# Batch 1's q and k loaded in runs of 72 tokens

## The chip, the cores and the metric

One core of a Trainium2 chip runs the whole program. The time is device microseconds of one execution; a kernel's time is the median over its runs. The engines are TensorE (PE; its weight loads, which overlap its matmuls, are listed as PEld), Vector (DVE), ScalarE (ACT), GpSimd (POOL) and SyncE (SP). Data moves between memory and the core by DMA, issued here from GpSimd's queue (all loads that change type on the way, fp32 to bf16) and from SyncE's.

## The reference

Causal attention with a forget-like bias, then a token mixer of rank 32 and a two-layer channel mixer. Inputs q, k, v are (8, 8, 576, 64): batch, heads, tokens, head size.

```python
scores = scale * np.matmul(q, k.transpose(0, 1, 3, 2))
s_pos = np.maximum(s, 0.0)
cum = np.cumsum(s_pos, axis=-1)
bias = -(cum[:, :, :, None] - cum[:, :, None, :])
scores = np.where(causal, -1000000000.0, scores + np.minimum(bias, 0.0))
attn = softmax(scores)                      # by rows, + 1e-09 in the sum
x = (attn @ v) as (batch, token, 512)
xt = x.transpose(0, 2, 1)
h = xt @ U @ V                              # (512, 576) @ (576, 32) @ (32, 576)
u = x + h.transpose(0, 2, 1)
return u + np.maximum(u @ w_ch1, 0.0) @ w_ch2
```

## The kernel before

The attention goes by pairs of heads: pair n = 4b + hp is pair hp of batch b, and there are 32. A pair has three steps, each a generator that is advanced piece by piece. `transposes(n)`, T_n for short, turns q and k of the pair: TensorE multiplies [72 x 128] pieces by an identity into PSUM, and copies (L337 or L340) bring them to a buffer `slot`, head size along the partitions, tokens along the free axis. `scores(n)`, S_n, multiplies k by q from the slot into PSUM (L404), ScalarE takes the exponential (L419, L430, L436) into `pT`, and a mask sets the causal part to zero. `values(n)`, V_n, multiplies pT by v (L464) and divides by the sum of the row (L473, L474). `seqmix(b)`, M_b, is the token mixer of one batch, and `chanmix(g)` the channel mixer for 512 tokens, with its first product on line L650 and its second on L660 or L699.

TensorE is kept busy by filling the attention's waits with pieces of `chanmix`. From pair 4 to pair 9 the order is written out by hand as words: "T4 T4", then "S4 T5 S4 T5 ...", then "V4 V4 S7 V5 ..." and so on, a piece of `chanmix` between them at a set pace. From pair 8 on it comes from a loop. In the end the order of TensorE's and GpSimd's instructions is fixed as written. Vector's, ScalarE's and SyncE's orders are fixed through batch 0 alone; after that a scheduler sets them.

How q and k come in. One tile of q and one of k per batch, 72 partitions x 8 heads x 512 numbers, with two buffers in turn. `load_qk(b, h, n)` loads n heads from h on, q and k each by one DMA from GpSimd's queue. `in_runs(b, h)` says which of two forms it takes, and the copies of `transposes` ask it too.

- In rows (L119): partition p holds tokens 8p to 8p + 7. For one head these lie side by side in memory, 2,048 B of fp32, and are written as 1,024 B of bf16. Turned on TensorE, the tokens come out in steps of 8, and the copies (L340) put each into its place: the source is read in steps of 72 elements, and every second element of the destination is written.
- In runs (L114): partition p holds tokens p, 72 + p, 144 + p and so on. Each piece is one token, 256 B of fp32 written as 128 B. Turned, each of the eight groups is a run of 72 tokens in their order, and the copies (L337) read and write runs of 72.

Before the change, batch 0, batch 1 and heads 0 to 3 of batch 2 are loaded in rows, heads 4 to 7 of batch 2 and all later batches in runs.

Where batch 1's loads stand. GpSimd issues in the order written. Heads 0 to 3 of batch 1 (q, then k) are issued at about 17.2 us, after the masks of pair 0 and before the masks of pair 1, w1's second half (L270), and the masks of pairs 2 and 3. Heads 4 to 7 are issued at about 25.8 us, after those masks; then follow w2's first half (L275), batch 1's v in five parts (L188), w2's second half, batch 2's q and k in two halves, and batch 2's v. The consumers of these on TensorE: T4 at 34.5 us, T6 at 43.5, the second product of `chanmix(0)` (L660) from 50.7, V4 at 53.0, T8 at 61.0.

Of the kernel before, what the change touches and what calls it, by code (L numbers as in the profile page):

```python
# [39 lines left out]
def kernel(  # L40
# [15 lines left out]
    B, H, S, D = q.shape  # L56
# [49 lines left out]
        k_t[b] = loads.tile([TP, H, TT * D], BF16, tag="k_sd", name="k_sd")  # L106

    def in_runs(b, h):
        return b > 2 or b == 2 and h >= 4

    def load_qk(b, h, n):
        for dst, src in ((q_t[b], q), (k_t[b], k)):
            if in_runs(b, h):
                nc.gpsimd.dma_start(  # L114
                    out=dst[:, ds(h, n), :].rearrange("p h (t d) -> p (h t) d", t=TT),
                    in_=src[b, ds(h, n)].rearrange("h (t p) d -> p (h t) d", p=TP),
                )
            else:
                nc.gpsimd.dma_start(  # L119
                    out=dst[:, ds(h, n), :],  # L120
                    in_=src[b, ds(h, n)].rearrange("h (p t) d -> p h (t d)", p=TP),
                )
# [173 lines left out]
    def transposes(n):  # L296
# [30 lines left out]
        for hh in range(2):  # L327
            if b > 0:
                turn(hh, 0)
            turn(hh, 1)  # L330
            tp = tps[hh]
            dst = slot[0:D, hh, 0 : 2 * S]
            for par in range(2):
                src = tp[par * D : par * D + D]
                if in_runs(b, 2 * hp):
                    by_run = dst.rearrange("p (c t two m) -> p c t two m", c=2, t=4, two=2)
                    copies(n, hh, par)(by_run[:, :, :, par, :], src)  # L337
                else:
                    in_turn = dst.rearrange("p (c m t two) -> p c m t two", c=2, t=4, two=2)
                    copies(n, hh, par)(  # L340
                        in_turn[:, :, :, :, par], src.rearrange("p c t m -> p c m t")
                    )
            yield
# [854 lines left out]
    for n in range(2 * PB, NP + 2):  # L1198
        b, hp = divmod(n, PB)
# [97 lines left out]
```

The softmax here doesn't subtract the row's maximum and nothing guards it: scores larger than these inputs give would overflow.

## Time and profile before

| | before |
|---|---|
| median of 14 runs | 363.35 us (362.35 to 369.06) |
| the profiled execution | 365.19 us |
| its span | 363.5 us |
| granted TensorE clock | 1.0 throughout |
| GpSimd's DMA queue | 110,016 packets, 18.50 MB |
| SyncE's and ScalarE's DMA queue | 44,760 packets, 18.64 MB |
| copies of turned q and k, L340 | 29 on Vector, 11 on ScalarE |
| copies of turned q and k, L337 | 76 on Vector, 12 on ScalarE |

The span runs from the first to the last instruction of the profiled execution; what lies around it makes the execution's time. Durations and points of time in this text come from that one execution. Sizes of DMA packets are those written, so bf16 where the load changes type. A DMA's row in the trace covers its issue on the engine; when its data has landed is told beside it.

### The profile page before, as it was taken

To read this page: it belongs to the slowest core of one execution; us is meant where nothing else is said; L and a number is where in the kernel's file an instruction comes from. 1 tells how busy PE (TensorE), PEld (TensorE's weight loads), DVE (VectorE), ACT (ScalarE), POOL (GpSimd) and SP (SyncE) were. 2 spreads that over 40 slices of the span, in tenths; PEclk is the share of its full clock that TensorE was granted. 3 is DMA by queue.
4 is the path that set the end of the run, shared out by engine and by line. 5 is a ranking of instruction groups with operands and counts; after the bars stand their busy time and mean duration, and the time that the engine had idled before them with its cause. 6 is when DMAs were issued, how large, how long until landed. Compare 5 with 4: busy or idle time off the path is not lost.

```text
span 363.5 us, 9613 instructions
## 1 busy us (share of the span) xinstructions
PE 350.4 (96%) x3999; PEld 256.9 (71%) x4039; DVE 276.4 (76%) x604; ACT 213.1 (59%) x322; POOL 84.9 (23%) x108
## 2 busy tenths in 40 slices
PE   8999999999997999999999999999899999999996
PEld 4675566665586667886689667876588548888885
DVE  7876776778787758995799659995697769676674
ACT  3874975846761577347853677348743554675710
POOL 8997161714040402140224003000000000000000
PEclk9999999999999999999999999999999999999999
DMA  7999999999999799959993999254222716010022
GB/s 108 163 195 202 160 178 132 153 143 126 96 108 105 144 132 70 107 76 131 131 85 70 149 148 86 50 119 81 6 29 72 150 20 127 29 60 31 30 88 87
DMA packets 155107, 37.94 MB, mean 104 GB/s; under 512 B 138680, under 2 KB 153432, under 8 KB 155064
## 3 DMA queue, kind: packets, MB, share of 16 engines
q0 software_dynamic: 110016, 18.50, 83.6%
q1 hardware_dynamic: 44760, 18.64, 31.2%
q8 instruction: 31, 0.51, 0.6%
q10 hardware_dynamic: 288, 0.20, 0.2%
q14 instruction: 12, 0.10, 0.1%
HBM read 37.25 MB, written 9.70 MB: 129 GB/s over the span
## 4 chain that ended last, share of the span: by engine, by line
PE 77%; DVE 11%; ACT 4%; DMA 3%; issue 3%; DVEq 0%; ACTq 0%
PE pwork L650 21%; PE pwork L699 11%; PE quarter L699 10%; PE pscore L404 9%; PE pwork L464 7%; PE parts L911 6%; PE pwork L317 4%; PE pwork L660 3%; DMA xT<-x_sb 3%; DVE uT L518 2%; DVE slot L677 2%; ACT hT L1000 2%; ACT pT L419 1%; DVE slot L340 1%; DVE o_sb L713 1%
## 5 line engine op out<-in xcount | busy, mean ns | idle before, releaser
L650 PE MATMUL pwork<-uT,w_sb 128*128 128x512 bf16 x401 | 105.9, 379 | 2.6 <-ACT hT L1000 0.9
L1000 ACT ACTIVATE hT<-pwork 128x512 bf16<-128x512 f32 x108 | 65.1, 607 | 38.4 <-PE pwork L650 38.1
L419 ACT ACTIVATE pT<-pscore 128x1024 bf16<-128x1024 f32 x56 | 56.5, 1029 | 50.8 <-PE pscore L404 50.0
L650 PEld LDWEIGHTS <-w_sb 128*128 128x128 bf16 x448 | 38.3, 98 | 35.9 <-issue 1.3
L404 PE MATMUL pscore<-slot 68*128 68x320 bf16 (+1 forms) x500 | 55.2, 246 | 0.2
L404 PEld LDWEIGHTS <-slot 68*128 68x128 bf16 x564 | 41.2, 97 | 17.0 <-issue 1.3
L699 PEld LDWEIGHTS <-hT 128*128 128x128 bf16 x496 | 46.3, 98 | 7.0 <-DVE uT L518 0.5
L188 POOL DMA_DIRECT2D v_slot<-in_v_dram x36 | 30.3, 854 | 78.3 <-PE pwork L464 67.1
L349 DVE TENSOR_TENSOR pT<-pT,keep 128x512 bf16<-128x512 bf16 (+1 forms) x81 | 28.6, 354 | 21.8 <-ACT pT L419 16.0
L464 PEld LDWEIGHTS <-pT 128*128 128x128 bf16 x870 | 32.4, 98 | 8.0 <-issue 2.9
L337 DVE COPY slot<-pwork 64x576 bf16<-64x576 bf16 x76 | 34.4, 453 | 4.6 <-PE pwork L317 3.7
L464 PE MATMUL pwork<-v_slot,pT 128*128 128x65 bf16 x870 | 35.5, 193 | 2.3 <-DVE uT L518 2.2
L474 DVE TENSOR_TENSOR x_sb<-pwork,rec 128x320 bf16<-128x320 f32 x64 | 31.2, 489 | 1.4
L430 ACT ACTIVATE pT<-pscore 128x1024 bf16<-128x1024 f32 x29 | 30.2, 1041 | 1.7 <-PE pscore L404 1.5
L699 PE MATMUL pwork<-w_sb,hT 128*128 128x256 bf16 x240 | 30.6, 273 | 0.0
L340 DVE COPY slot<-pwork 64x576 bf16<-64x576 bf16 x29 | 23.3, 803 | 5.3 <-PE pwork L317 3.5
L699 PEld LDWEIGHTS <-slot 128*128 128x128 bf16 x256 | 24.0, 98 | 4.6 <-issue 1.6
L114 POOL DMA_DIRECT2D q_sd<-in_q_dram x6 | 12.6, 2107 | 48.2 <-PE pwork L317 35.5
L473 DVE RECIPROCAL rec<-pwork 128x5 f32<-128x5 f32 x64 | 12.1, 190 | 12.7 <-PE pwork L464 12.4
L699 PE MATMUL pwork<-w_sum,slot 128*128 128x256 bf16 x160 | 20.3, 273 | 0.7 <-DVE o_sb L713 0.7
L317 PEld LDWEIGHTS <-q_sd 72*128 72x128 bf16 x256 | 14.8, 99 | 8.6 <-DMA q_sd<-in_q_dram 0.9
L317 PE MATMUL pwork<-identity,q_sd 72*128 72x72 bf16 x256 | 18.2, 198 | 0.1
(165 smaller groups left out, 544.5 us busy)
## 6 DMA issues: line engine op xcount, KB each, us to landing
out_dram<-o_sb SPq DMA_DIRECT2D x35, 256.0 KB
w_sb<-in_moe_w_ch_dram POOLq DMA_DIRECT2D x4, 1024.0 KB, 13.6
v_slot<-in_v_dram POOLq DMA_DIRECT2D x28, 128.0 KB, 10.2
q_sd<-in_q_dram POOLq DMA_DIRECT2D x5, 576.0 KB, 15.4
k_sd<-in_k_dram POOLq DMA_DIRECT2D x5, 576.0 KB, 20.1
q_sd<-in_q_dram POOLq DMA_DIRECT2D x4, 288.0 KB, 13.2
k_sd<-in_k_dram POOLq DMA_DIRECT2D x4, 288.0 KB, 12.8
q_sd<-in_q_dram POOLq DMA_DIRECT2D x4, 144.0 KB, 4.9
```

Of the source, the lines that this page charges most:

```text
L188: nc.gpsimd.dma_start(out=vt[:rows_t, t, :, 0:D], in_=v[b, :, ds(t * 128, rows_t), :].rearrange("h p d -> p h d"),)
L317: nc.tensor.transpose(tps[hh][:, c, t2, :], src[:, 2 * hp + hh, ds(t2 * 128, 128)], identity[:TP, :TP],)
L337: copies(n, hh, par)(by_run[:, :, :, par, :], src)
L349: nc.vector.tensor_tensor(dst, dst, keep[:, :, 0:w].to_broadcast([128, n_tiles, w]), op=ALU.min)
L404: nc.tensor.matmul(dst, lhsT=slot[0:KA, hh, ds(S + j * 128, 128)], rhs=slot[0:KA, hh, lo:hi], start=True, stop=True,)
L419: nc.scalar.activation(pT[:, hh, 0:1024], near, EXP, scale=scale)
L430: nc.scalar.activation(pT[:, :, 1024:1536], mid.rearrange("p (a b) -> p a b", a=2), EXP, scale=scale)
L464: nc.tensor.matmul(po[:, i, :], lhsT=pT[:, hh, ds(place(j, i), 128)], rhs=vt[:, j, h, :], start=(j == 0), stop=(j == i), skip_group_check= ...
L474: nc.vector.tensor_tensor(x_sb[:, hp, :, ds(hh * D, D)], po[:, :, 0:D], rec.to_broadcast([128, 5, D]), op=ALU.mult,)
L650: nc.tensor.matmul(f1, lhsT=w1_sb[:, kt, ds(nf * 128, 128)], rhs=u[:, kt, :], start=(kt == 0), stop=(kt == 3),)
L699: nc.tensor.matmul(acc[:, i, :], lhsT=a[:, kt, ds(i * 128, 128)], rhs=b[:, kt, :], start=(begin and i == 0 and kt == 0), stop=(kt == HF - ...
L1000: nc.scalar.activation(hT[:, nf, :], f1, RELU)
```

## The change

`in_runs` answers yes for all of batch 1 as well. Heads 0 to 3 of batch 2 stay in rows, as batch 0 does.

```diff
     def in_runs(b, h):
-        return b > 2 or b == 2 and h >= 4
+        return b in (1, *range(3, B)) or b == 2 and h >= 4
```

So four DMAs (q and k of heads 0 to 3 and of heads 4 to 7 of batch 1) go from line L119 to L114, each from 288 pieces to 2,304 for the same bytes, and the sixteen copies of T4 to T7 go from L340 to L337. The instructions on TensorE and on GpSimd, and their order, are otherwise the same. On Vector the scheduler puts some of its work around these copies in another order: the three copies of V_sb (L1190), which stood after T4's copies, and the four of V_end (L1191), which stood before them, both come after them, and some masks (L349) change places with the copies of T5 to T7. On SyncE two small transfers of bias rows (L301) change places.

## The prediction

> **What bounds the kernel now.** I read the page's engine row first, then the loads' rates and landings, then the chain and Vector's rows in the stage of the change.
>
> ```profile
> PE 350.4 (96%) x3999; PEld 256.9 (71%) x4039; DVE 276.4 (76%) x604; ACT 213.1 (59%) x322; POOL 84.9 (23%) x108
> DMA  7999999999999799959993999254222716010022
> 34.00:56.00 22.00, 21.52 (x231) 13.36 (x234) 16.35 (x31) 18.62 (x29) 9.47 (x13) 1.00 1.62 174
> ```
>
> TensorE is busy 96% of the span; the DMA digits (slices of 9.1 us) stand at nine from about 9 to 118 us. The third line is the windows view for 34 to 56 us, where batch 1's heads are turned, scored and multiplied: PE idles 22.00 - 21.52 = 0.48 us there, so no cheaper Vector work can give back more than that in this stage. The last figures are a DMA share of 1.62 (over one: packets overlap) and 174 GB/s: the GpSimd queue always has a transfer in hand.
>
> What the edit buys is the price of a copy out of PSUM, L340 (row form) against L337 (run form):
>
> ```profile
> L340 DVE COPY slot<-pwork x29: 786/804/820, 8.3 to 69.1; 64x576 bf16<-64x576 bf16 x29
> L337 DVE COPY slot<-pwork x76: 439/454/459, 78.4 to 267.8; 64x576 bf16<-64x576 bf16 x76
> 52.69 1.63 DVE L340 COPY slot<-pwork 64x576 bf16<-64x576 bf16 x2
> 54.37 1.02 PE L660 MATMUL pwork<-w_sb,hT 128*128 128x512 bf16 x4 [0.26 <-DVE slot L340]
> ```
>
> Minimum/median/maximum are ns. The last two lines are the timeline: the only named TensorE wait on these copies between 34 and 62 us is 0.26 us.
>
> What it costs is seen in the DMA view of two stretches, batch 1's second half (row form, 33.0 to 36.9 us) and batch 2's second half (run form, 58.7 to 64.9 us), and in the landings of the two k loads that bound the second.
>
> ```profile
> DMA packets 853, 0.76 MB, mean 195 GB/s; under 512 B 119, under 2 KB 852, under 8 KB 852
> DMA packets 6152, 0.69 MB, mean 111 GB/s; under 512 B 6146, under 2 KB 6152, under 8 KB 6152
> L119 POOL DMA_DIRECT2D k_sd<-in_k_dram x1: 719/719/719, 43.6 to 43.6; - x1
> DMA to landing us min/median/max: 15.1/15.1/15.1
> L114 POOL DMA_DIRECT2D k_sd<-in_k_dram x1: 1407/1407/1407, 47.8 to 47.8; - x1
> DMA to landing us min/median/max: 17.2/17.2/17.2
> 61.15 0.29 PE L317 MATMUL pwork<-identity,k_sd 72*128 72x72 bf16 x4
> ```
>
> The first number of a landing line is how long after the issue the data was there. The row loads ran at 195 GB/s, the run loads at 111, in the bf16 bytes written. Batch 2's first k half, in rows, landed at 43.6 + 15.1 = 58.7 us; TensorE first reads it at 61.15 us (T8). That slack, 61.15 - 58.7 = 2.4 us, is the number everything turns on. Two other loads are as near: the fifth part of batch 1's v, issued at 33.6, takes 16.8 us to land (50.4 us), and V4 starts at 52.96 us; the second half of w2 lands at 35.7 + 19.5 = 55.2 us and is first wanted near 58.7 us (the seventeenth L660 matmul).
>
> **The change, part by part.** No instruction is added, removed or moved on TensorE; the order on GpSimd is the same too.
>
> Copies. Batch 1 has T4 to T7 with 4 copies each: 14 on Vector, 2 on ScalarE (L340's rows between 34 and 56 us count 14 and 2). Vector saves 14 x (805 - 454) ns = 4.9 us; ScalarE 2 x (798 - 634) ns = 0.3 us. What hides this is TensorE's own work. I take the 0.26 us of the named wait, bounded by 0 and 0.48 us. Vector's order shifts with the scheduler (the three V_sb copies go behind T4's), which has the same cover.
>
> Issues on GpSimd. Four issues change from L119 to L114. A run issue of four heads took 1.43 and 1.41 us, a row issue 0.77 and 0.72: +0.67 us each. The first pair is issued at 17.2 us with no gap to the masks behind it: masks of pT(1), a memset, a w1 load, masks of pT(2) (22.46 to 23.9) and pT(3) (to 25.8) all slide by up to 1.35 us. V2 starts on TensorE at 25.5, where its masks would now end near 25.3; V3 starts at 27.1, its masks would end near 26.9 because the third of them stood 0.29 us waiting for ScalarE. So 0.1 us, bounded by 0 and 0.4. Behind the second pair (25.8 us) stand w2's first half and v of batch 1, 2.5 us later in issue; their landings lie 16 us after issue, behind other transfers, so this costs nothing unless the queue ran dry.
>
> Transfers. Each of the four loads moves the same bytes: 72 partitions x 4 heads as 288 packets of 1,024 B become 2,304 of 128 B. A q and k pair in rows cost the queue, from the landing ahead of it to that of its k: batch 1's second (w1's half at 21.6 + 11.4 = 33.0, k at 26.5 + 10.4 = 36.9) 3.9 us, batch 2's first (w2's half at 55.2, k at 58.7) 3.5, batch 1's first (w1's half at 23.9, k at 17.9 + 9.5 = 27.4) 3.5: mean 3.6. A pair in runs, batch 2's second: 47.8 + 17.2 = 64.9 less 58.7, 6.2 us. So +2.6 us a pair, and D = 5.2 us of delay from two pairs for all that is queued behind. Bounds: batch 4's full k load, the same packets as a pair, landed 4.3 us after its q (86.3 + 23.8 less 84.0 + 21.8), giving +0.7 a pair and D = 1.4; batch 3's (65.9 + 17.8 less 63.5 + 13.2) 7.0 us after its q, giving +3.4 and D = 6.8. The rates say the like of the middle: 294,912 B at 195 and at 111 GB/s are 1.5 and 2.7 us, times four +4.6. I take 5.2, from the same shape in the same queue, nearest in time.
>
> What is late. The first halves would land near 30 us against T4 at 34.5, the second near 42 against T6 at 43.5: no wait. Then all slack is spent. Batch 1's last v part: 50.4 + 5.2 = 55.6 against some 53.3 us (it feeds the last of V4's first fifteen matmuls), a stall of 2.3; w2: 60.4 against 58.7 + 2.3, none; T8's k: 63.9 against 61.15 + 2.3, another 0.5. These are one delay, not three: together D - 2.4 = 2.8 us (0 to 4.4 by the bounds of D), and all of TensorE's order stands behind the waiting matmul, with Vector and ScalarE, which wait for its products. The queue issues one transfer only when the eighth before it has landed (w2's second half, at 35.7, waited for q of batch 1, landed 35.4), so the delay is not made up at the issue.
>
> Afterwards. Batch 3's k lands at 83.7 us against T12 at 88.3: 4.6 us of slack, of which 2.4 would be used. At 105.4 us the last transpose of batch 2's x stands 9.76 us on the chain, TensorE idles 2.24 us for it, and the GpSimd queue works beside it until 118 us. If the loads, 2.4 us later relative to TensorE, push it back, it costs up to 2.4 more; if the two share as before, nothing. I take 0, and 2.4 for the range. After 118 us the queue stands empty until 124, so lateness ends there, but a TensorE stall stays: it idles only 223.0 - 217.1 = 5.9 us in the last 223.
>
> Sum: +2.8 - 0.3 + 0.1 = +2.6 us. The profiled execution is 365.19 us (span 363.5 and 1.7 around it), so 367.8 for its like; it lies 1.84 above the median of the 14 runs, and on 363.35 the sum is 365.9.
>
> A rule to weigh. The Trainium skill, "DMA: Bandwidth & Descriptors", section "Anatomy of one DMA — SWDGE (gpsimd) path", fits a transfer as 2 us plus its bytes over 436 GB/s, whatever its pieces. By that fit rows and runs cost alike, D is 0 and the sum would be some 363.2 us. The same page's "Specifications" ask at least 512 B a transfer for line rate, which speaks against the change. The 195 and 111 GB/s above side with the second, and they decide.
>
> **The rivals.**
>
> Hidden: the delay fits the slack. For it: 2.4 us are free, and batch 4's and 5's k loads come 4.3 and 4.8 us after their q, giving D = 1.4 and 2.4. Against it: those compare landings deep in a backlog, where engines have run ahead. Then TensorE keeps its pace and gains 0 to 0.48: 362.9 to 363.4 us. This is the case that isn't slower; it decides as long as D stays under 2.4.
>
> Doubled: TensorE stalls 2.8 to 4.4 us and the transpose at 105 us is pushed by a further 1 to 2.4. For it: between 106 and 110 us the queue's loads ran and the transpose hardly did. Against: the loads it meets are issued on TensorE's own progress. 363.35 + 2.6 + 1 to 363.35 + 4.2 + 2.4: 367.0 to 370.0 us.
>
> Reordered, faster: the later backlog lets that transpose go first; its 2.24 us wait goes and nothing stalls before. 363.35 - 0.3 - 2.24 = 360.8 us at best. Nothing in the rows asks for it except that 9.76 us is long.
>
> That the change does nothing is excluded: the four issues and sixteen copies carry the other lines.
>
> **How the numbers follow.** The forecast, a stall of 1 to 4.4 us at V4 and T8: 0.57, 364.2 to 367.6 us (363.35 - 0.2 and the stall). Hidden: 0.18. Doubled: 0.17. Reordered: 0.08. The predicted time is the forecast's: 365.9 us. From 363.0 to 368.8 lies all of the first, most of hidden and of doubled; below lie the faster case and the rest of hidden (0.11), above the rest of doubled (0.06). By itself the likeliest case spans 364.2 to 367.6. A measurement of this kernel can tell 0.2%, 0.7 us, from no change: faster means under 362.6, slower over 364.1. Slower is the first and third, 0.74, with a hair of hidden, 0.75; same, most of hidden, 0.15; faster 0.10.
>
> **What would show it.** Right: batch 1's k landings some 2.5 and 5 us later than 27.4 and 36.9 us; batch 2's first k at about 64 us; TensorE waiting for a DMA by name, at V4 or T8, in a stretch where it had none; the copies at 455 ns. Wrong: no DMA wait there (the step D fails), masks on GpSimd holding V2 or V3 (the 0.1 fails), or a gain in 34 to 56 us over 0.48 us, which would mean that TensorE's modelled busy time hides waits on Vector.

## The result, and the profile after

| | before | changed |
|---|---|---|
| median | 363.39 us (48 runs, 362.24 to 370.87) | 368.83 us (10 runs, 366.9 to 370.83) |
| ratio, 95% interval | | 1.0144 [1.0117, 1.0171] |
| the profiled execution, its span | 365.19, 363.5 us | 367.53, 365.8 us |
| GpSimd's DMA queue | 110,016 packets, 18.50 MB | 120,768 packets, 18.51 MB |

The kernel became 5.2 us slower (0.0144 x 363.4; the medians lie 5.4 us apart). The forecast had the direction and half the size. Ratios, here and below, leave out executions that took over 1.5% more than the fastest of the same kernel.

One profiled execution of each is not enough to see where 5 us went, because single executions of one kernel differ by 1 to 2 us. The profiled execution of the kernel before, which the prediction worked on, lay 1.84 us above its median. A second one, taken with the experiments (called "before again" here), took 362.74 us with a span of 361.0 us and serves as the base from here on.

The page of the changed kernel: engines, DMA digits, the run copies of q and k.

```profile
PE 350.3 (96%) x3999; PEld 256.6 (70%) x4039; DVE 271.2 (74%) x604; ACT 212.9 (58%) x322; POOL 87.7 (24%) x108
DMA  7999999999999599939992999244222706010022
L337 DVE COPY slot<-pwork 64x576 bf16<-64x576 bf16 x90 | 40.8, 453 | 6.9 <-PE pwork L317 5.8
```

TensorE does the same 3,999 matmuls in the same busy time (350.3 against 350.4 us). Vector did save what the copies promised: 276.4 - 271.2 = 5.2 us, with 14 more run copies (76 to 90) of 453 ns. None of it shows in the time.

The windows view of the changed kernel, then of before again: busy us (and count) of PE, PEld, DVE, ACT, POOL; then the granted clock, the DMA share, GB/s.

```profile
26.00:31.00 5.00, 3.50 (x72) 2.97 (x70) 3.39 (x12) 1.17 (x2) 4.94 (x8) 1.00 1.57 189
34.00:56.00 22.00, 20.61 (x212) 12.59 (x215) 11.53 (x32) 18.45 (x29) 8.69 (x12) 1.00 2.06 142
63.00:70.00 7.00, 5.54 (x77) 3.78 (x78) 4.77 (x12) 3.78 (x5) 1.78 (x2) 1.00 3.42 137
100.00:120.00 20.00, 18.31 (x239) 15.19 (x237) 16.95 (x40) 9.41 (x14) 4.24 (x5) 1.00 2.52 111
```

```profile
26.00:31.00 5.00, 4.54 (x78) 3.53 (x75) 3.15 (x11) 1.43 (x3) 4.62 (x9) 1.00 1.14 213
34.00:56.00 22.00, 21.74 (x240) 13.39 (x237) 16.84 (x32) 18.68 (x29) 10.20 (x13) 1.00 1.65 174
100.00:120.00 20.00, 19.72 (x272) 16.89 (x271) 18.06 (x43) 8.09 (x13) 5.54 (x6) 1.00 1.59 116
```

TensorE lost about a microsecond in each of these stretches: 4.54 - 3.50 at V3, 21.74 - 20.61 around V4, 19.72 - 18.31 at the transpose of batch 2's x, and 7.00 - 5.54 = 1.46 of idle time at T8. In the stage from 34 to 56 us the load rate fell from 174 to 142 GB/s.

What TensorE waited for in those places, by the view of its waits (total, times, longest), changed kernel:

```profile
PE pwork L464 <- issue: 1.4, 1, 1.4
PE pwork L464 <- DVE uT L518: 1.4, 1, 1.4
PE pwork L317 <- DMA k_sd<-in_k_dram: 1.3, 1, 1.3
PE pwork L464 <- DMA v_slot<-in_v_dram: 1.1, 1, 1.1
```

and before again, between 20 and 120 us:

```profile
PE pwork L464 <- issue: 0.5, 1, 0.5
PE pwork L464 <- DVE uT L518: 0.2, 1, 0.2
```

Two waits for DMA by name are new: V4's for v of batch 1 and T8's for k of batch 2. The wait called "issue" (for nothing that the profile shows) is V3's last matmul, at 28.5 to 29.7 us. The one for uT is V12 behind the last transpose of batch 2's x. On the timeline of the changed kernel:

```profile
29.71 0.19 PE L464 MATMUL pwork<-v_slot,hT 128*128 128x65 bf16 x1 [1.44 <-issue]
...
55.16 1.07 PE L464 MATMUL pwork<-v_slot,pT 128*128 128x65 bf16 x21 [1.07 <-DMA v_slot<-in_v_dram]
...
64.31 0.30 PE L317 MATMUL pwork<-identity,k_sd 72*128 72x72 bf16 x4 [1.29 <-DMA k_sd<-in_k_dram]
...
118.91 0.62 PE L464 MATMUL pwork<-v_slot,pT 128*128 128x65 bf16 x15 [1.39 <-DVE uT L518]
```

Landings, each from the issue and the time to landing beside it, as in this row of the changed kernel for batch 1's second k (28.3 + 13.5 = 41.8 us):

```profile
L114 POOL DMA_DIRECT2D k_sd<-in_k_dram x1: 1416/1416/1416, 28.3 to 28.3; - x1
...
DMA to landing us min/median/max: 13.5/13.5/13.5
```

| landed at, us | before | before again | changed | changed less before again |
|---|---|---|---|---|
| batch 1's first k | 27.4 | 28.9 | 29.6 | 0.7 |
| batch 1's second k | 36.9 | 36.6 | 41.8 | 5.2 |
| w2's first half | 43.0 | 42.5 | 48.8 | 6.3 |
| last part of batch 1's v | 50.4 | 50.1 | 55.5 | 5.4 |
| batch 2's first k | 58.7 | 58.4 | 64.2 | 5.8 |
| batch 3's k | 83.7 | 83.0 | 89.4 | 6.4 |

From batch 1's second k on the delay in the queue is 5 to 6 us and stays. The lateness of TensorE is smaller and comes in steps. The following table gives when an instruction of TensorE starts, less the same start in before again; "changed 2" and "changed 3" are two more profiled executions of the changed kernel, "loads only" an experiment below.

| us late at | before again starts it at | before | changed | loads only | changed 3 | changed 2 |
|---|---|---|---|---|---|---|
| T4 | 34.1 | 0.4 | 1.2 | 0.7 | 0.9 | 0.7 |
| V4, second head | 53.1 | 0.4 | 2.5 | 2.7 | 3.5 | 12.0 |
| T8, k | 60.8 | 0.4 | 3.6 | 3.5 | 4.5 | 11.6 |
| T12 | 87.8 | 0.4 | 3.6 | 3.5 | 4.5 | 11.6 |
| V12 | 114.2 | 2.5 | 4.8 | 4.5 | 5.9 | 11.6 |
| end | 361.0 | 2.5 | 4.8 | 4.5 | 5.9 | 11.5 |

All of the loss is made before 120 us, and after that the columns don't move. In the three columns that are alike (changed, loads only, changed 3) it is made in three places: 0.7 to 1.2 us before T4, then 2.3 to 3.7 from there to T8, then 1.0 to 1.4 at V12. Part of the first is older than the change. The first changed load is issued at 16.9 to 17.1 us; the scores' matmuls that before again starts at 15.83 us, ahead of that, start 0.6 us late in loads only and in changed 3, and 0.2 us late in changed. Loads only, then before again:

```profile
15.51 0.62 PE L404 MATMUL pscore<-slot 68*128 68x128 bf16 x6 [0.30 <-DMA slot<-hT]
16.39 0.60 PE L404 MATMUL pscore<-slot 68*128 68x128 bf16 x6
...
15.83 0.61 PE L404 MATMUL pscore<-slot 68*128 68x128 bf16 x6
```

The transfer waited for (slot<-hT) is issued from SyncE's queue before 13.5 us.

### The profile page after: what moved, and what is told of

It reads as the page before. It is cut to its first block, busy times and chain, and to the rows that moved or that the text cites. A ratio compares the mean times of both kernels' runs of the same rounds, so it can differ in the third digit from the quotient of the medians.

```text
span 365.8 us, 9612 instructions
## 1 busy us (share of the span) xinstructions
PE 350.3 (96%) x3999; PEld 256.6 (70%) x4039; DVE 271.2 (74%) x604; ACT 212.9 (58%) x322; POOL 87.7 (24%) x108
## 3 DMA queue, kind: packets, MB, share of 16 engines
q0 software_dynamic: 120768, 18.51, 85.9%
## 4 chain that ended last, share of the span: by engine, by line
PE 74%; DVE 10%; DMA 9%; ACT 4%; issue 3%; SPq 0%; DVEq 0%; ACTq 0%
PE pwork L650 21%; PE pwork L699 11%; PE quarter L699 10%; PE pscore L404 8%; PE pwork L464 7%; PE parts L911 6%; DMA k_sd<-in_k_dram 4%; PE pwork L317 3%; DMA xT<-x_sb 2%; DVE uT L518 2%; PE pwork L660 2%; DVE slot L677 2%; ACT hT L1000 1%; DMA slot<-hT 1%; ACT pT L419 1%
## 5 line engine op out<-in xcount | busy, mean ns | idle before, releaser
L349 DVE TENSOR_TENSOR pT<-pT,keep 128x512 bf16<-128x512 bf16 (+1 forms) x81 | 28.7, 354 | 23.7 <-ACT pT L419 16.0
L337 DVE COPY slot<-pwork 64x576 bf16<-64x576 bf16 x90 | 40.8, 453 | 6.9 <-PE pwork L317 5.8
L114 POOL DMA_DIRECT2D q_sd<-in_q_dram x8 | 15.5, 1940 | 48.4 <-PE pwork L317 34.7
L317 PE MATMUL pwork<-identity,k_sd 72*128 72x72 bf16 x256 | 17.9, 198 | 1.4 <-DMA k_sd<-in_k_dram 1.3
L699 PE MATMUL quarter<-w_sb,hT 128*128 128x256 bf16 x144 | 18.0, 273 | 0.3 <-DVE uT L518 0.3
```

Of the source, the lines that this page charges most:

```text
L317: nc.tensor.transpose(tps[hh][:, c, t2, :], src[:, 2 * hp + hh, ds(t2 * 128, 128)], identity[:TP, :TP],)
L349: nc.vector.tensor_tensor(dst, dst, keep[:, :, 0:w].to_broadcast([128, n_tiles, w]), op=ALU.min)
L699: nc.tensor.matmul(acc[:, i, :], lhsT=a[:, kt, ds(i * 128, 128)], rhs=b[:, kt, :], start=(begin and i == 0 and kt == 0), stop=(kt == HF - ...
```

## The experiments

**The four parts side by side.** The changed kernel again (changed 2); the loads alone; the copies alone; the kernel before again.

```diff
# loads only, in load_qk
-            if in_runs(b, h):
+            if b == 1 or in_runs(b, h):
# copies only, in transposes
-                if in_runs(b, 2 * hp):
+                if b == 1 or in_runs(b, 2 * hp):
```

In each of the two the loads and the copies of batch 1 disagree on the form, so the tokens of batch 1's q and k come out in another order; the instructions are otherwise those of the two kernels.

> The changed kernel again, for a second trace and a second interval. In the first pair of traces only 2.3 us of the 5.4 us between the medians are to be seen: 0.8 at a TensorE pause near 29 us that has no named cause, 1.4 at V4 (v of batch 1), 1.5 at T8 (k of batch 2), 0.5 won back beside V4 by cheaper copies, 0.8 won back at the transpose wait near 110 us. The delay theory expects the same places with other sizes, the waits at V4 and T8 together 3 to 6 us, and a ratio of 1.012 to 1.017. The rival, that what the trace does not show lies in the later part (after 120 us), expects T8 as before and a gap that grows after it.

> Batch 1 is loaded in runs, but its copies stay those of the row form, so its tokens stand in another order and the attention of batch 1 is that of shuffled tokens. Same transfers as the changed kernel, without the cheaper copies. The delay theory expects the whole loss and a little more, 1.013 to 1.019. The rival, that the copies and the order that the scheduler gives Vector and SyncE with them cost time, expects 1.000 to 1.005.

> Batch 1 is loaded in rows as before, but its copies are those of the run form, so its tokens stand in another order here too. The cheaper copies alone. The delay theory expects 0.998 to 1.000: at most 0.5 us, the idle time of TensorE between 34 and 56 us. The rival (copies and order) expects most of the loss here, 1.008 or more.

> The kernel before against itself, for a second trace and the noise of the comparison: 1.000 within 0.002. Its first profiled execution lay 1.84 us over its median. If that time sat in the waits near 29 and 110 us, this trace shows them shorter; if it sat outside the span or all over, the waits stay at 0.6 and 2.2 us.

Measured: the changed kernel 1.0169 [1.0137, 1.0201], loads only 1.0136 [1.0103, 1.0169], copies only 0.9999 [0.9980, 1.0018], before again 1.0001 [0.9987, 1.0014]. So the loads carry the whole loss, and the copies give nothing. Loads only shows the same waits as the changed kernel, by the view of TensorE's waits from 34 to 120 us:

```profile
PE pwork L464 <- DMA v_slot<-in_v_dram: 1.7, 2, 1.4
PE pwork L464 <- DVE uT L518: 1.2, 1, 1.2
PE pwork L317 <- DMA k_sd<-in_k_dram: 0.9, 1, 0.9
```

In the trace of copies only, TensorE reached T8 1.0 us earlier than in before again, 0.6 of it between T4 and T8, and had lost it all at V12, by a wait of 1.3 us for uT. That place, which the prediction had priced at nothing, can take time without any of the changed loads.

The profiled execution of changed 2 (374.28 us) shows something the first had not. First its waits, then its windows from 44 us, columns as above:

```profile
PE pwork L317 <- DMA k_sd<-in_k_dram: 8.7, 1, 8.7
```

```profile
44.00:48.00 4.00, 0.02 (x1) 0.00 (x0) 0.00 (x0) 0.99 (x2) 0.00 (x0) 0.98 1.53 127
48.00:52.00 4.00, 0.00 (x0) 0.00 (x0) 0.00 (x0) 0.00 (x0) 0.00 (x0) 0.50 1.93 82
52.00:56.00 4.00, 3.29 (x16) 1.70 (x17) 1.67 (x4) 1.30 (x2) 0.75 (x1) 0.50 2.78 134
56.00:60.00 4.00, 4.00 (x24) 2.11 (x23) 0.91 (x2) 2.40 (x4) 2.41 (x3) 0.74 1.31 204
```

Batch 1's second k, issued at 28.1 us, landed at 52.7 instead of 41.8. T6 stood 8.7 us for it, and the granted clock was then half for some 10 us. "The second near 42 against T6 at 43.5: no wait" held in the other executions, and failed here. After it nothing waited for loads, and nothing at V12.

**One half of batch 1 alone, and batch 2.**

```diff
# first half, second half, batch 2 in rows, batch 1 in runs and batch 2 in rows
-        return b > 2 or b == 2 and h >= 4
+        return b > 2 or b == 2 and h >= 4 or b == 1 and h < 4
+        return b > 2 or b == 2 and h >= 4 or b == 1 and h >= 4
+        return b > 2
+        return b > 2 or b == 1
```

> Heads 0 to 3 of batch 1 in runs, heads 4 to 7 in rows. Half of the delay, D = 2.6 us, against 2.4 us of slack at T8. The delay theory with a threshold expects a third or less of the loss, 0 to 1.5 us: 1.000 to 1.004, of it up to 0.8 us at the pause near 29 us. A loss that is proportional to the packets would be 2.6 us, 1.007; a loss by the masks on GpSimd that slide behind the first pair of issues would show whole here, 1.010 or more.

> Heads 4 to 7 of batch 1 in runs, heads 0 to 3 in rows. Half of the delay again, no slide of the masks. The delay theory expects 0 to 1.5 us as with the first half, 1.000 to 1.004, without the longer pause near 29 us. A loss that is proportional to the packets: 1.007. If the loss is made by the first pair of issues: 1.000 or below.

> Batch 1 as before, and all of batch 2 in rows: two run loads fewer than before. They lie behind T8's loads in the queue, so TensorE had no wait on them. If lateness of the queue is what makes the transpose wait near 110 us, it shortens by up to 2 us and the kernel is faster than before, 0.994 to 0.998. If that wait has nothing to do with the queue's lateness, the dearer copies at T10 and T11 cost 0 to 0.5 us: 1.000 to 1.002.

> Batch 1 in runs as in the changed kernel, all of batch 2 in rows: as many run loads as before, but two pairs ahead of T8's loads and none behind. The delay theory expects the loss of the changed kernel at V4 and T8 nearly whole, since the loads that wait there stand behind batch 1's: 1.008 to 1.016. The rival, that the sum of small packets up to 120 us sets the time wherever they stand, expects half of the loss: with one pair more in runs ahead and one pair fewer behind, 1.003 to 1.007.

Measured: first half 1.0062 [1.0021, 1.0102], second half 1.0069 [1.0038, 1.0101]. A threshold would have left each of them nearly free, because one pair's delay of 2 to 3 us fits the slack of 2.4. It is not so: 0.0062 + 0.0069 = 0.0131, the whole loss in two shares. The waits say why. First half, from 20 to 120 us:

```profile
PE pwork L464 <- DVE uT L518: 1.7, 1, 1.7
PE pwork L464 <- issue: 1.2, 1, 1.2
```

Second half, from 34 to 120 us:

```profile
PE pwork L464 <- DVE uT L518: 1.5, 1, 1.5
...
PE pwork L464 <- DMA v_slot<-in_v_dram: 0.2, 1, 0.2
PE pwork L317 <- DMA k_sd<-in_k_dram: 0.2, 1, 0.2
```

At V4 and T8 the threshold holds: no wait, or 0.2 + 0.2. But at V12 TensorE waits 1.5 to 1.7 us, against 0.2 in before again, as if the slack that was used at V4 and T8 were missed there. How far the change makes this wait is taken up below.

Batch 2 in rows came out at 1.0027 [0.9992, 1.0061], no gain, where one theory had expected one and the other 1.000 to 1.002; its profiled execution had half the clock from 13 to 34 us, so its stages can't be read. Batch 1 in runs with batch 2 in rows: 1.0142 [1.0082, 1.0202], as slow as the changed kernel, though batch 2's second half was now cheap. So it does not help to have fewer small packets behind V4 and T8; those ahead of them are enough for the whole loss.

**Is it the meeting with u's transpose?** Between 34 and 50 us SyncE's queue turns u of the first 512 tokens. These two kernels leave that transpose out and add h's buffer in place of u to the first 512 output rows, so that part of the output is not the reference's.

```diff
# both: in the first group of chanmix
-            if nf == (3 if g > 0 else NF - 1):
+            if g > 0 and nf == 3:
...
-                u_sd[:, :, i, :],
+                first_hT[:, 0:4, 0:128],
```

> The changed kernel without the DMA transpose of u for the first 512 tokens, which SyncE issues at 34 us: the outputs of these tokens get other numbers added in place of u. In the second trace of the changed kernel k of batch 1, heads 4 to 7, landed at 52.7 us in place of 41.7, TensorE stood 8.7 us for it at T6 and fell to half clock for 10.2 us; between 38 and 50 us the DMA engines took one packet of the transpose for one of the loads. If the small packets' meeting with this transpose makes the delay and its scatter, the loss against the kernel before falls to 0 to 2 us here, 1.000 to 1.005, with no run over 368. If the rate of the small packets alone makes it, the waits at V4 and T8 stay as they were and the ratio is 1.010 or more.

> The kernel before, without the same transpose, for the comparison with the run beside it. TensorE waited for no load between 34 and 100 us, so nothing is won there: 0.996 to 1.001. If the run beside it is near 1.012 and this one near 1.000, the transpose is no part of the cause.

Measured: the changed kernel without that transpose 1.0022 [0.9991, 1.0052], the one before without it 1.0000 [0.9968, 1.0032]. The loss is nearly gone, but not for the reason I had in mind. The last part of v landed at 51.6 against 46.6 us, batch 1's second k at 41.1 against 36.3: the delay is still 5 us. What the missing transpose did was to free the queue of some 3.5 us in both kernels (v at 50.1 in before again, 46.6 here), and so to raise the slack at V4 and T8 from 2.4 to about 6 us. The delay now fits: no wait for a load is left in the trace of the changed kernel without the transpose. V12 still waited, 1.7 us. So the loads in runs make the delay without the transpose, and the slack decides what it costs at V4 and T8. That reading of mine, that meeting the transpose makes the delay, fell. The scatter is another matter: three of the changed kernel's six executions beside the first experiments took 374 us or more, and none of these 12 over 368.21. The greater slack may hide it, or it may need the transpose; no run tells which. Nor does a run separate the slower packets from the longer issues. GpSimd issued w2's first half 2.7 us later in the changed kernel (29.67 against 26.97 us), and it landed 6.3 us later.

**Lateness without small packets.** The kernel before, with 0.9 MB of w2 loaded once more in 1,024 B pieces into spare buffers, behind the loads of batch 1's q and k; nobody reads them.

```diff
     load_qk(1, 4, 4)
+    nc.gpsimd.dma_start(out=spare_x, in_=spare_in[:, 0:5, :])
+    nc.gpsimd.dma_start(out=spare_u[:, 0:2, :], in_=spare_in[:, 5:7, :])
```

> The kernel before with 0.9 MB of w2 loaded a second time into spare room, in pieces of 1,024 B, right behind batch 1's second q and k: by the rates of before some 5.3 us more of the queue's time for everything behind, and no small packets. If lateness of the queue alone makes the loss, TensorE waits 2 to 4 us at V4 and T8, and the ratio is 1.006 to 1.012. The pause near 29 us stays near 0.5 us, T6 does not wait, and few runs lose more. If it is the small packets as such (their meeting with the transpose, with the fetch of instructions), the ratio stays under 1.004.

Measured: 1.0089 [1.0055, 1.0123], some 3.2 us. A queue that is late by other work costs time too, in rows and with the old copies, though less than the 5.2 us of the change. Its profiled execution had half the clock from 13 to 26 us, so its stages can't be compared with those of the others, and where an execution at full clock loses the 3.2 us isn't seen. In this one T12 waited 1.8 us for batch 3's k and V12 1.3 us for uT: T12's wait is lateness paid at a later consumer of the same queue.

**The next batch's v later.** The loads of v for the next batch compete with the last transpose of x; here they are issued one pair later, from batch 2 on.

```diff
-        if hp == 0 and 2 <= b < B - 1:
+        if hp == 1 and 2 <= b < B - 1:
```

> The kernel before, with v of batches 3 to 6 issued one pair of heads later, so that batch 4's v no longer runs beside the last transpose of batch 2's x near 105 us. That transpose took 9.8 us in the first trace of before (TensorE waited 2.2 us), and TensorE waited 0.2 us in the second. If the v loads beside it make its wait, it stays at 0.2 us or less: 0.997 to 1.001. If batch 4's q and k do, nothing changes.

> The changed kernel with the same later v. Its first trace had 1.4 us of wait for that transpose, the halves 1.7 and 1.5. If the loads that are late at that point make it, the wait goes to 0.2 us and the ratio falls by 0.003 to 0.004, to 1.009 to 1.013. If the wait comes of batch 4's q and k, it stays: 1.013 to 1.017.

Measured: on the kernel before 0.9994 [0.9962, 1.0026], on the changed one 1.0157 [1.0086, 1.0228], no gain in either. On the kernel before the wait at V12 was the longest of any run:

```profile
PE pwork L464 <- DVE uT L518: 2.5, 1, 2.5
```

So that wait doesn't need v's loads beside the transpose. The trace of the changed one had half the clock from 12 to 22 us, which moved all that follows; its 0.4 us at V12 tells nothing.

**A third trace of each.** One profiled execution more of the changed kernel (changed 3) and of the one before.

> A third trace of the changed kernel, for where its time goes in an execution that is neither the shortest nor the longest: waits at V4 and T8 of 2 to 4 us together, at the pause near 29 us 0.8 or more, at the transpose 0.2 to 1.7; and, if the granted clock is below 1.0, its low stretch right after the longest of these waits.

> A third trace of the kernel before, beside it: no wait for a load, the pause near 29 us 0.5 to 0.6, the transpose wait 0.2 (as in the second trace) or 2.2 (as in the first).

Changed 3: 368.67 us, span 367.0. Before: 364.5 us, span 362.8. Changed 3's windows around V4, columns as above:

```profile
52.00:56.00 4.00, 1.90 (x20) 1.15 (x19) 1.48 (x5) 1.23 (x3) 3.54 (x5) 1.00 2.42 149
56.00:60.00 4.00, 3.83 (x38) 2.46 (x38) 1.37 (x4) 0.00 (x0) 2.74 (x5) 0.57 1.24 206
```

V4 waited 2.2 us in two pieces, the longer 1.4; then the clock was half for 3.4 us, and by T8 TensorE had fallen a further 1.06 us behind. At V3 it waited 0.7 us, not the 0.8 or more that was expected, at V12 1.6. The kernel before had this, from 20 to 120 us:

```profile
PE pwork L464 <- issue: 1.6, 1, 1.6
...
PE pwork L464 <- DVE uT L518: 0.2, 1, 0.2
```

So the pause at V3 can be long without the change. V3's last matmul is late more often with it: with batch 1's first half in runs by 0.7, 0.7, 0.9, 0.9, 0.9, 0.9 and 1.2 us against before again (seven traces); with it in rows by -0.6, -0.4, -0.2, 0.0, 0.4 and 1.7 (six). Left out on both sides are traces with a low clock before that point. But in five of the seven (changed 2, changed 3, loads only, the changed kernel without u's transpose, batch 1 in runs with batch 2 in rows) TensorE was 0.6 to 0.9 us late already at the matmuls near 16 us, ahead of the first changed load, and between there and V3's last matmul it changed by -0.2 to 0.3. In four of the five it had waited there for the transfer slot<-hT, 0.3 to 0.9 us, in changed 3 for ScalarE, 0.6. Only in changed and in first half was the lateness made later, 1.0 and 0.8 us; in the third trace of the kernel before it was 1.1.

No kernel beat the kernel before; copies only, late v and the kernel without u's transpose are level with it.

## Why the prediction was half right, and where it failed

**The copies: right.** Taken at -0.26 us; copies only measured 0.9999, and TensorE's own work hid the rest. The 0.6 us that TensorE gained before T8 in that trace lies a little above the bound of 0.48, and was lost again at V12.

**The issues on GpSimd: not shown to cost anything.** Taken at 0.1 us, bounded by 0 and 0.4. The masks did slide: GpSimd issues batch 1's second q at 26.8 us, in before again at 25.6. But V3 doesn't wait for them by name, the profile calls its wait "issue", and most of the lateness at V3 was there before the first changed load was issued (five of seven traces, above). The 1.0 and 0.8 us of the other two stand beside 1.1 in a trace of the kernel before. Nor would this time come on top of the rest: up to T8 it is part of one sum, as shown below.

**The transfers: right.** D was put at 5.2 us and measured 5.4 at v's last part and 5.8 at batch 2's first k. The bounds, 1.4 to 6.8, held. Batch 1's k loads and batch 2's first k, forecast near 30, 42 and 64 us, landed at 29.6, 41.8 and 64.2.

**What is late: right in place, somewhat small.** The forecast was D - 2.4 = 2.8 us at V4 and T8, split as 2.3 and 0.5. The waits by name made 1.1 + 1.3 = 2.4 in the changed kernel, 1.7 + 0.9 = 2.6 in loads only. In before again the slack at T8 was 60.75 - 58.4 = 2.3 us; the k came 5.8 later, and TensorE was late there by 3.56, which is about the difference (3.5). So in changed and in loads only, whatever is lost before T8, at 16 us, at V3 or at V4, is part of one sum that the landing of this k sets: 3.5 us, where the terms of the forecast (2.8 - 0.3 + 0.1) made 2.6. T6 waited for its k in one trace of these loads, changed 2, by 8.7 us, and in no other.

**Afterwards: this step failed.** "If the loads, 2.4 us later relative to TensorE, push it back, it costs up to 2.4 more; if the two share as before, nothing. I take 0, and 2.4 for the range." Against before again, the runs gave 1.0 to 1.4 us at V12 in the three traces that are alike, and 1.5 and 1.3 of lateness there with half the change (first half, second half). The rival called doubled had a further 1 to 2.4 us there, and comes nearest to the traces. Its argument against, "the loads it meets are issued on TensorE's own progress", does not hold: in thirteen of the seventeen traces batch 4's q was issued 0.3 to 0.4 us after batch 3's k had landed, in before at 84.0 after 83.7, in before again at 83.4 after 83.0, in changed at 89.8 after 89.5. In the other four it was 0.6 to 2.1 us, and V12 waited no more than 0.2 us in them. So in most executions these loads go by the queue's progress, and keep its lateness.

The table has the landing of batch 4's k less the issue of that transpose, and how much later V12 began than in the shortest case, 9.14 us after that issue. "More rows of w2" is the kernel of lateness without small packets.

| trace | lag of batch 4's k, us | V12 later by, us |
|---|---|---|
| batch 2 in rows | -3.9 | 0 |
| batch 1 in runs, batch 2 in rows | -2.7 | 0 |
| before, third | 0.7 | 0 |
| before again | 1.9 | 0 |
| changed, late v | 3.6 | 0.2 |
| changed 3 | 4.2 | 1.4 |
| copies only | 4.2 | 1.1 |
| more rows of w2 | 4.5 | 1.2 |
| second half | 4.6 | 1.4 |
| before | 4.7 | 2.1 |
| changed without u's transpose | 4.9 | 1.5 |
| loads only | 5.0 | 1.0 |
| changed | 5.3 | 1.2 |
| first half | 6.5 | 1.5 |
| before, late v | 7.3 | 2.3 |

Up to 3.6 us of lag there is no wait to speak of; from 4.2 on there is one of 1 to 2.3 us. (In changed 2 and in the kernel before without u's transpose, V12 was on time too; the landing isn't in their records.) Two numbers go together in fifteen traces, which is no proof: no kernel was run with batch 4's q and k taken from beside the transpose. And the wait is not the change's own. Of six traces with all of batch 1 in rows and no long stretch of low clock, three have it, of 1.3, 2.2 and 2.5 us (copies only, before, late v on before), and three do not. Of the traces with batch 1 or half of it in runs all six that were without a low stretch of over 6 us have it, 1.2 to 1.7 us. So the change seems to make common what was there in some executions before. In batch 1 in runs with batch 2 in rows the traced execution, at half clock for 6.8 us, had no wait there, and the two at full clock took 367.2 and 367.5 us, hardly less than the changed kernel's.

**The base was off, too.** The sum was made on an execution that had a wait of 2.1 us at V12 in it already, by the table above, while before again and the third trace had none. Against that execution V12's wait did not grow at all (1.4 us after, 2.2 before), so "I take 0" fits it. Moving the sum to the median, 1.84 us lower, then set it on executions without that wait, and left out what V12 adds to them. Before again lies 0.65 us under the median of 363.39 itself, so for a typical execution the 1.2 us at V12 are rather an upper figure.

**A term was missing: the clock after a wait.** Of 18 executions of the changed kernel, 13 had a mean granted clock under 0.999; of the kernel before, 20 of the 96 beside the four sets of experiments (1 of 23, 12 of 30, 3 of 26 and 4 of 17, each set on another chip). Among the changed kernel's five at full clock the median is 367.7 us, 4.8 over the 362.9 of the kernel before at full clock beside changed 2, and as much as the traces' three places make (365.8 - 361.0 = 4.8). The other 0.6 us up to 5.4 would then go with the lower clock and with the scatter of batch 1's second k; this is argued, not shown. Nor does each low clock follow a wait of this kind: in three traces (batch 2 in rows, more rows of w2, the changed kernel with late v) it fell between 11 and 14 us, ahead of all of them.

So, in round numbers from the traces and against before again: 3.5 us up to T8 (2.6 forecast), 1.2 at V12 (0 forecast), some 0.6 more, perhaps with the clock (not thought of). The step that failed is "Afterwards: I take 0"; the stall behind D was a smaller miss. Open are what makes the lateness near 16 us, what V3's last matmul waits for, why batch 1's second k lands between 41.8 and 52.7 us in the same kernel, and the cause of the step at V12.

## What to carry to other kernels

Slack at the next consumer need not be spent for free where the queue stays backlogged (each half of the change waited 0 to 0.4 us for loads, and cost 0.6 to 0.7%): follow the lateness to the point where the queue runs empty, and price every later place where a transfer is near its consumer. Before a sum is built on one profiled execution, compare it with the median; if it is above, find which wait makes it so, because the change may bring that wait to executions that were without it. Before lateness is put down to a change, see whether it was there ahead of the first instruction that the change touches. A cheaper copy on an engine with spare time is worth nothing against eight times as many packets on a queue that has none.

## What the runs showed of the hardware

**Small packets beside a DMA transpose.** While u's transpose ran, both queues moved about as many packets as each other, whatever they carried (before again 352 and 349 from 38 to 40 us, when the loads moved 0.29 MB; 766 and 766 from 42 to 44 us, when they moved 0.10 MB). The DMA view of the changed kernel from 46 to 50 us; q1 is SyncE's queue, q0 GpSimd's (packets, MB, share of 16 engines):

```profile
q1 hardware_dynamic: 941, 0.23, 86.5%
q0 software_dynamic: 1145, 0.16, 81.2%
```

0.16 MB in 4 us are 40 GB/s for the loads in 128 B packets. From 42 to 44 us, with packets of 1,024 B, the same meeting left them about 150 GB/s (313 packets against 313). That would explain how a load of small packets that meets a transpose can become very late, as in changed 2; it is argued from these counts, and no run tried it alone.

**Half the clock after short waits.** The low stretches were 3.4 us long in changed 3, 6.8 in batch 1 in runs with batch 2 in rows, 10.2 in changed 2. The first came behind waits of 2.2 us in all, none longer than 1.4, in a window of 4 us where TensorE was busy for 1.90; the second behind 2.6 us in all at V4, none longer than 1.4. Loads only waited 1.7 us there, the longest again 1.4, and kept the full clock. The Trainium skill, "TensorE: Matmul & The Clock Gate", section "Part 1: The HAM clock gate (the "warmup" mystery)", has the clock halved after one idle window of about 3.4 us. The 8.7 us wait agrees with it: the clock fell 3.8 us after it began. The waits of 1.4 us do not, if each is taken for itself. In changed 3 it was enough that TensorE was idle for half of 4 us.
